# The backward pass of an S4 block: first output finished in the last stage, K's gradient inverted ahead of W2's first parts, and two small preparations moved into the wait for K

## The chip, the cores and the metric

The kernel is one launch on one core of one Trainium2 chip. The metric is device time in microseconds of that launch; the median over the runs shown is compared. TensorE, VectorE, ScalarE, GpSimd and SyncE appear in the profile as PE (PEld for its weight loads), DVE, ACT, POOL and SP.

## The reference

The forward pass is a normalised input, a convolution with a long kernel K made from the parameters of a state space model, and a two-layer feed-forward gate. The kernel returns the forward output and the gradients of eleven inputs for a given `grad_out`.

```python
xn = _layernorm(x)                            # x: 1 x 2048 x 512, bf16
K  = einsum("dn,dnl,dn->dl", C, exp(dt*A*l), dt*B).real        # N = 128 states, l = 0..2047
s  = irfft(rfft(xn, 4096) * rfft(K, 4096))[:2048] + xn * Dskip
g  = silu(silu(xn @ w1) @ w2)                 # w1: 512 x 1792, w2: 1792 x 512
out_0 = x + s * g
out_1 .. out_11 = gradients of x, A_re, A_im, B_re, B_im, C_re, C_im, log_dt, Dskip, w1, w2
```

## The kernel before

Everything works on tiles of 128 partitions. The sequence of 2048 is held as `[128, T=16, 512]` (16 positions to a partition), and the transform of length 4096 is done as matrix products with tables (TF for the forward direction, TI for the inverse, both written to DRAM once and loaded in pieces) and radix-4 additions on VectorE (`rad4`). Spectra have four parts, kt = 0 to 3, each `[128, 2, 4, 512]` (real and imaginary, 1 MB).

The instructions stand in the order in which the Python code issues them; there is no planner. Each engine runs its own list in order, and so does each of the three queues that issue transfers (SyncE, ScalarE, GpSimd); a transfer that waits holds everything behind it on its queue. Pools recycle buffers: a load into a buffer waits for the last reader of what was there. Transfers of SyncE and ScalarE take turns on eight semaphores, so that each also waits for the one eight before it.

- **Stage 1** runs the feed-forward net and makes the tables. It stores the gate's two forms (`gd`, `od`) and fills DS = grad_out * g.
- **Stage 2** makes K through DRAM (`store_K`, `load_K` into `K_b`) and the spectra of xn (`UXd`) and of part 3 of DS. While K's loads are under way it does the last products on VectorE and transposes on TensorE. Its end opens the pools `kq` and `bk3`, starts the generator `gen_kt` and finishes BK3, the part 3 of K's gradient before the inverse.
- **Stage 3** steps `gen_kt`: for each kt, K's spectrum KX (stored to `KXd`), the product with UX, and `rad4` into BY. Beside its first steps it drains `sl`, the transposes of the last slab (`XT`, `YT`). At its end 64 matmuls (L1199) form `ps_dsk`, the sums for Dskip's gradient.
- **Stage 4** inverts BY in eight steps of two (`inv_mm`, L1101). `YOut.load` fetches four operands a step: co, cG, cg, cx. `YOut.pre` makes cG = grad_out times silu' (DSILU on ScalarE, L133, and a product, L1236). `YOut.out` has three VectorE operations: DO_all = S * cG (L1242), S *= cg (L1243), S += cx (L1244), and S_s is stored as out_0 (L1307). Between the steps `gen_d` makes the spectra XD of DS for kt 0 to 2 (stored to `DXd`), the products with UX, and BK0 to BK2. Late in the stage GpSimd loads the first three pieces AW of the hidden layer (`akd`) for W2's gradient, and `Prod` loads KXd and DXd of part 0 (aXl, dXl; L1419, L1421).
- **Stage 5** begins with the selection matrices (`gsum_sel`: iotas on GpSimd, 4 casts and 7 comparisons on VectorE) and three parts of W2's gradient (`Dw2.run`, L1453), which contract over all 16 tiles of DO_all. Then come eight steps of K's inverse (`inv_mm` over BK, `ps_v`), each evicted to dK by ScalarE (L1491) and summed with the selection matrices into `ps_g` (L1485). Beside them VectorE does the products and `rad4` of `Prod` for kt 0 to 3, into BG. The sums go to DRAM (`dKgd`, L1512 and L1513, two buffers `gs_o`) and come back as Gt by GpSimd loads (L1522, L1523). After W2's part 3 and the first three steps of DXC (the inverse of BG), the slabs begin: Gbd (L1606) from Gt and masks, `ps_V` (L1618) with loaded XTl, and so on, between W2's other parts, DXC's other steps and the transposing loads of W2T.
- **Stage 6** goes back through the feed-forward net and ends with W1's gradient: four chunks of `dhd` loaded by GpSimd as dhc (1792 KB each, L1813, two buffers), four sums of 16 matmuls to each (L1840), evicted and stored as o10b.

The step of stage 5 that changes most, as it is written:

```python
    for ft in range(3):
        for _ in w2.run(ft):
            pass
    ...
    for t0 in range(0, T, TS):
        ps = k.pd.tile([P, TS, W], F32, name="ps_v", tag="pd")
        inv_mm(k, ps, k.BK, k.TI.pop(t0), t0, (0, 1, 2, 3))
```

Of the kernel before, what the change touches and what calls it, by code (L numbers as in the profile page):

```python
# [14 lines left out]
P = 128  # L15
# [121 lines left out]
def kernel(ctx, tc, A_u, A_A_re, A_A_im, A_B_re, A_B_im, A_C_re, A_C_im, A_log_dt, A_Dskip, B_x, B_w1, B_w2, grad_out,  # L137
# [16 lines left out]
    LD = lambda nm: dr.tile([L, D], BF16, name=nm)  # L154
    k.gd = LD("gd"); k.od = LD("od")
    k.Kud = dr.tile([NU, D], BF16, name="Kud")
# [775 lines left out]
def stage_2(k):  # L932
# [89 lines left out]
    UX = ld_ux(k, kq, 0)  # L1022
    bk3 = lo.open("bk3")
    gk = gen_kt(k, kq, K_b, UX)
    next(gk)
    k.BK3 = rad_inv(k, bk3, "BK3", PX)
    return gk, sl

# [76 lines left out]
def gsum_sel(k, gp):  # L1105
# [6 lines left out]
    for (v0, st, u0, na, nb, reps, at) in (  # L1112
# [4 lines left out]
        nu = P if nb else 1  # L1117
        ii = gp.tile([P, nu], I32, name=f"gs_i{u0}")
        nc.gpsimd.iota(ii[:], pattern=[[st, nb], [128, na], [8, 16]] if nb else [[0, 1]], base=v0, channel_multiplier=0)
        iv = gp.tile([P, nu], BF16, name=f"gs_v{u0}")  # L1120
        nc.vector.tensor_copy(out=iv[:], in_=ii[:])
# [52 lines left out]
def stage_3(k, gk, sl):  # L1174

    nc = k.nc
    lo, ro = k.left, k.right
    for n, _ in enumerate(gk, 1):
        for g in (next(sl, None) for _ in range(2)):
            if g is not None:  # L1180
                next(g)
        if n == 7:
            ro.close("sb", "xs")
            k.tip = ro.open("tip", 3); k.y2 = ro.open("y2", 2)
            y = k.y = YOut(k)
# [10 lines left out]
    psd = k.psd = k.ps.tile([P, DK, P], F32, name="ps_dsk", tag="pz", bufs=1)  # L1196
    for kt in range(4):
        for t in range(T):
            nc.tensor.matmul(out=psd[:, kt], lhsT=k.DS[:, t, kt * P:(kt + 1) * P], rhs=k.xn[:, t, kt * P:(kt + 1) * P], start=(t == 0), stop=(t == T - 1))  # L1199

# [13 lines left out]
class YOut:  # L1214
# [23 lines left out]
    def out(self, t0, S_s):  # L1238
        k, nc, r = self.k, self.k.nc, self.ins.pop(t0)
        ts_ = slice(t0, t0 + TS)  # L1240
        TT = nc.vector.tensor_tensor
        TT(out=k.DO[:, ts_, :], in0=S_s[:], in1=r["cG"][:], op=ALU.mult)  # L1242
# [9 lines left out]
def gen_d(k, bk, dp):  # L1252
# [4 lines left out]
    for kt in range(3):  # L1257
# [21 lines left out]
def stage_4(k):  # L1279
# [9 lines left out]
    for t0 in range(0, T, TS):  # L1289
# [18 lines left out]
        for _ in range(3 if t0 % 4 else 2):  # L1308
            next(gd, None)
        if t0 == 4:  # L1310
            dskb = dskip_out(k, k.kq)
# [97 lines left out]
class Prod:  # L1409


    def __init__(self, k):
        self.k, self.ld, self.pl = k, {}, [(k.kq, "A", k.kq, "X")]

    def load(self, kt, src):
        k, nc = self.k, self.k.nc
        p0, t0, p1, t1 = self.pl[kt % 2]
        a = p0.tile([P, 2, 4, W], BF16, name="aXl", tag=t0)
        nc.sync.dma_start(a[:], src[kt])  # L1419
        d = p1.tile([P, 2, 4, W], BF16, name="dXl", tag=t1)  # L1420
        nc.sync.dma_start(d[:], k.DXd[kt])  # L1421
        self.ld[kt] = a, d

    def mul(self, kt):
        k = self.k
        a, d = self.ld.pop(kt)
        self.PX = cplx_mul(k.nc, k.mm, a, d, conj_a=True)

    def rad(self, kt, B_):
        k = self.k  # L1430
        t = k.mm.tile([P, 2, 4, W], BF16, name="r4_t", tag="cm_t2")
        E, O = (t[:, i].rearrange("p (c m) w -> p c m w", c=2) for i in range(2))
        rad4(k.nc, B_[:, :, 0:2], B_[:, :, 2:4], self.PX, E, O, True)
# [29 lines left out]
def stage_5(k):  # L1463
# [5 lines left out]
    pr = k.pr  # L1469
    pr.pl.append((k.kq, "UXl", pw, "dXl"))  # L1470
    pr.load(1, k.KXd)
# [16 lines left out]
    for t0 in range(0, T, TS):  # L1488
# [6 lines left out]
        else:  # L1495
            k.TI[t0 + 6 - T] = ld_ti(k, k.tip, t0 + 6 - T)
        kt = (t0 + 2) // 4
        if t0 % 4 == 0:
            pr.rad(kt, BG[:, kt])
        elif kt < 4:  # L1500
            pr.mul(kt)
        if t0 < 4:
            pr.load(t0 // 2 + 2, k.KXd)
        if t0 >= 2:
            gs(t0 - 2)
    gs(T - 2)
    for _ in gen_masks(k, dkp):
        pass
    g0 = k.dKgd[0:256].rearrange("(b p k) d -> k p b d", p=16, k=2)
    for i, (u0, nu, _) in enumerate(sels):  # L1510
        ob = dkp.tile([P, D], BF16, name=f"gs_o{i}", tag=f"gs_o{i % 2}")
        nc.scalar.copy(out=ob[0:nu], in_=(psg + [psz])[i][0:nu])  # L1512
        nc.sync.dma_start(k.dKgd[u0:u0 + nu], ob[0:nu])  # L1513
        if i < 2:
            nc.sync.dma_start(g0[i], dK[0:16, 8 * i:8 * i + 8])
    lo.close("bk", "bk3", "kq")
    S = Slabs(k, lo.open("sw"))
    S.load(0, nc.gpsimd); S.load(1, nc.gpsimd); S.load(2, nc.gpsimd)
    Gt = k.Gt = k.tf2.tile([P, 16, 256], BF16, name="Gt", tag="TFs")
    nc.gpsimd.memset(Gt[64:96], 0.0)  # L1520
    for e in range(2):
        nc.gpsimd.dma_start(Gt[e:79 + e:2], k.dKgd[0:640, 256 * e:256 * e + 256].rearrange("(h l) d -> h l d", l=16))  # L1522
        nc.gpsimd.dma_start(Gt[80 + e:81 + e, 0, :], k.dKgd[640:641, 256 * e:256 * e + 256])  # L1523
    for _ in w2.run(3):
# [269 lines left out]
def stage_6(k):  # L1794
# [5 lines left out]
    k.fx = ro.open("fx", 2)  # L1800
    fb = lo.open("fb", 2)
    B = k.B
    B.fb, B.W1T = fb, W1T
# [31 lines left out]
    for i in range(4):  # L1835
        for dk in range(DK):
# [18 lines left out]
    ro.close("fp4", "ww", "fx", "fw", "wt", "tip", "tf2", "tfp")  # L1855
    lo.close("fb", "do", "mm", "ds")

# [29 lines left out]
```

## Time and profile before

| what | value |
| --- | --- |
| runs | 820.08, 820.78, 816.17 us; median 820.08 |
| profiled execution | 818.51 us, span 816.7 us, mean granted clock 0.925 |
| PE busy | 675.6 us (83%) |
| DVE busy | 623.3 us (76%) |
| ACT busy | 435.4 us (53%) |
| POOL busy | 91.7 us (11%) |
| moved by DMA | 193.09 MB, mean 236 GB/s |
| stage 3 and 4 | about 305 to 460 us |
| K's inverse and sums | 469.4 to 516.1 us |
| first ps_V | 539.8 us |
| W1's sums | 754.8 to 812.8 us |

Busy time is of one execution, and matmuls overlap, so 83% does not mean that TensorE is at its peak. The span runs from the first to the last instruction of the profiled execution; its time is some 2 us longer. In timelines a row gives start, length, engine, line, operation, output<-inputs, count, and in brackets the idle time before it with what ended it. The tile called `ps_w2` or `ps_w1` in the code is `ps_w` in the profile, since numbers are left out.

### The profile page before, as it was taken

To read this page: it belongs to the slowest core of one execution; us is meant where nothing else is said; L and a number is where in the kernel's file an instruction comes from. 1 tells how busy PE (TensorE), PEld (TensorE's weight loads), DVE (VectorE), ACT (ScalarE), POOL (GpSimd) and SP (SyncE) were. 2 spreads that over 40 slices of the span, in tenths; PEclk is the share of its full clock that TensorE was granted. 3 is DMA by queue.
4 is the path that set the end of the run, shared out by engine and by line. 5 is a ranking of instruction groups with operands and counts; after the bars stand their busy time and mean duration, and the time that the engine had idled before them with its cause. 6 is when DMAs were issued, how large, how long until landed. Compare 5 with 4: busy or idle time off the path is not lost.

```text
span 816.7 us, 13686 instructions
## 1 busy us (share of the span) xinstructions
PE 675.6 (83%) x5284; PEld 345.5 (42%) x5284; DVE 623.3 (76%) x1013; ACT 435.4 (53%) x531; POOL 91.7 (11%) x124
## 2 busy tenths in 40 slices
PE   5878969896688557889999579959976899989998
PEld 3434535443456433334444234324433455444454
DVE  6899999639998994999889699745555548988700
ACT  5788888964679464434343112324533675666211
POOL 1251251020000030000000000401022200001010
PEclk9978989998889877989999689979988999999999
DMA  9557767799769499974789788759999597657561
GB/s 280 199 170 260 244 222 264 260 322 290 255 210 279 119 291 278 331 292 174 265 300 350 274 316 282 223 146 271 222 186 265 135 271 217 175 153 233 167 217 50
DMA packets 153806, 193.09 MB, mean 236 GB/s; under 512 B 37179, under 2 KB 114557, under 8 KB 147565
## 3 DMA queue, kind: packets, MB, share of 16 engines
q1 hardware_dynamic: 142780, 156.84, 62.5%
q0 software_dynamic: 6416, 22.30, 8.6%
q10 hardware_dynamic: 4545, 13.08, 5.3%
q8 instruction: 41, 0.67, 0.3%
q14 instruction: 24, 0.20, 0.1%
HBM read 108.01 MB, written 80.50 MB: 231 GB/s over the span
## 4 chain that ended last, share of the span: by engine, by line
PE 25%; DVE 12%; DMA 11%; ACT 4%; SPq 3%; issue 2%; POOL 0%; ACTq 0%; DVEq 0%
PE ps_w L1840 6%; PE ps_v L1101 4%; PE ps_f L1077 4%; DMA XTl<-XTd 3%; PE ps_dx L1763 3%; PE ps_w L1453 2%; PE ps_da L1724 2%; DMA dhd<-dhk 2%; DVE cm_t L106 1%; SPq L1566 1%; DMA dXl<-DXd 1%; PE ps_V L1618 1%; DMA TIs<-TId 1%; DMA TFs<-TFd 1%; ACT sd L133 1%
## 5 line engine op out<-in xcount | busy, mean ns | idle before, releaser
L579 PE MATMUL ps_h<-XNT,W 128*128 128x512 bf16 x224 | 60.3, 418 | 12.2 <-ACT hs L582 12.2
L1453 PE MATMUL ps_w<-DO_all,AW 128*128 128x512 bf16 x224 | 60.4, 421 | 10.2 <-DVE DO_all L1242 10.2
L555 PE MATMUL ps_o<-W,aT 128*128 128x512 bf16 x224 | 56.9, 405 | 2.5 <-DVE ak L76 2.5
L1101 PEld LDWEIGHTS <-TIs 128*128 128x128 bf16 x384 | 37.4, 99 | 49.6 <-issue 6.1
L1077 PEld LDWEIGHTS <-TFs 128*128 128x128 bf16 x304 | 30.4, 102 | 58.6 <-issue 23.6
L1077 PE MATMUL ps_f<-K_b,TFs 128*128 128x512 bf16 x160 | 42.0, 417 | 15.1 <-ACT Ak L1079 7.2
L1724 PE MATMUL ps_da<-DOT,W2T 128*128 128x512 bf16 x224 | 52.9, 379 | 1.5 <-ACT DOT L1704 1.1
L1620 ACT CAST Vb<-ps_V 128x1024 bf16<-128x1024 f32 x32 | 31.8, 1014 | 41.9 <-PE ps_V L1618 24.6
L1763 PE MATMUL ps_dx<-W1T,dhT 128*128 128x512 bf16 x224 | 52.9, 379 | 0.0
L1629 DVE TENSOR_TENSOR T<-Vb,YTl 128x2048 bf16<-128x2048 bf16 x16 | 19.6, 1224 | 42.4 <-ACT Vb L1620 42.4
L1725 DVE TENSOR_TENSOR dhT<-ps_da,sd 128x1024 bf16<-128x1024 f32 x28 | 34.1, 1222 | 23.0 <-ACT sd L133 17.3
L1840 PE MATMUL ps_w<-dhc,xn 128*128 128x448 bf16 x256 | 49.1, 352 | 0.0
L886 ACT COPY XT<-pt_xt 128x1024 bf16<-128x1024 bf16 (+1 forms) x44 | 40.6, 1004 | 5.0 <-issue 3.8
L1453 PEld LDWEIGHTS <-AW 128*128 128x128 bf16 x224 | 21.9, 105 | 44.0 <-issue 25.8
L1618 PE MATMUL ps_V<-XTl,Gbd 82*32 82x256 bf16 x512 | 20.8, 296 | 23.0 <-DMA XTl<-XTd 13.2
L579 PEld LDWEIGHTS <-W 128*128 128x128 bf16 x224 | 22.6, 105 | 37.4 <-issue 20.2
L927 PE MATMUL ps_f<-xn,TFs 128*128 128x512 bf16 x128 | 32.8, 412 | 5.8 <-DMA TFs<-TFd 5.8
L555 PEld LDWEIGHTS <-aT 128*128 128x128 bf16 x224 | 23.3, 104 | 33.6 <-issue 11.1
L1772 ACT ACTIVATE dxn<-dxn,c,rstd 128x512 f32<-128x512 f32 x16 | 13.0, 814 | 43.8 <-DVE c L1771 43.8
L1077 PE MATMUL ps_f<-DS,TFs 128*128 128x512 bf16 x144 | 33.0, 379 | 3.6 <-DMA TFs<-TFd 1.9
L1079 ACT CAST Ak<-ps_f 128x1024 bf16<-128x1024 f32 x16 | 16.0, 1014 | 37.2 <-PE ps_f L1077 21.2
L928 ACT CAST XU<-ps_f 128x1024 bf16<-128x1024 f32 x20 | 20.7, 1040 | 27.5 <-PE ps_f L927 14.5
(299 smaller groups left out, 1545.4 us busy)
## 6 DMA issues: line engine op xcount, KB each, us to landing
TIs<-TId SPq DMA_DIRECT2D x24, 512.0 KB, 7.2
XTd<-XT SPq DMA_DIRECT2D x20, 512.0 KB, 6.1
XTl<-XTd SPq DMA_DIRECT2D x13, 640.0 KB, 6.6
hTd<-hs SPq DMA_DIRECT2D x28, 256.0 KB, 2.4
akd<-ak SPq DMA_DIRECT2D x28, 256.0 KB, 3.7
UXl<-UXd SPq DMA_DIRECT2D x7, 1024.0 KB
hsb<-hTd SPq DMA_DIRECT2D x28, 256.0 KB, 3.2
dhd<-dhk SPq DMA_DIRECT2D x28, 256.0 KB, 5.3
```

Of the source, the lines that this page charges most:

```text
L555: nc.tensor.matmul(out=pso[:], lhsT=aT[:, ft, tt * P:(tt + 1) * P], rhs=W2[:, ft, :], start=(ft == 0), stop=(ft == FT - 1))
L579: nc.tensor.matmul(out=ps[:, j], lhsT=W1[:, dk, ft * P:(ft + 1) * P], rhs=XNT[:, dk], start=(dk == 0), stop=(dk == DK - 1))
L886: nc.scalar.copy(out=XT[:, j0:j0 + len(ks)], in_=pt[:, 0:len(ks)])
L927: nc.tensor.matmul(out=ps[:, c, :], lhsT=TFs[:, t1 + 4 * j, c, :], rhs=src[:, t1 + 4 * j, :], start=(j == 0), stop=(j == 3))
L1077: nc.tensor.matmul(out=ps[:, c, :], lhsT=tab(j), rhs=src[:, t1 + 4 * j, :], start=(n == 0), stop=(n == 4 * len(terms) - 1))
L1101: nc.tensor.matmul(out=ps[:, j, :], lhsT=TIs[:, j, 2 * kt + c, :], rhs=B[kt][:, c, (t0 + j) % 4, :], start=(kt == 0 and c == 0), stop=(kt ...
L1453: nc.tensor.matmul(out=ps[:], lhsT=A[:, t, :], rhs=k.DO[:, t, :], start=(t == 0), stop=(t == T - 1))
L1620: nc.scalar.copy(out=self.V[i][:, g2], in_=ps[:].rearrange("p b c n -> p c b n"))
L1724: nc.tensor.matmul(out=ps[:, j], lhsT=self.W2T[:, dk, ft * P:(ft + 1) * P], rhs=self.DOT[tc_][:, dk], start=(dk == 0), stop=(dk == DK - 1))
L1725: nc.vector.tensor_tensor(out=self.dhT[:, f0:f0 + 2, :], in0=ps[:], in1=sd[:], op=ALU.mult)
L1763: nc.tensor.matmul(out=psx[:], lhsT=dhT[:, ft, t % 4 * P:(t % 4 + 1) * P], rhs=self.W1T[:, ft, :], start=(ft == 0), stop=(ft == FT - 1))
L1840: nc.tensor.matmul(out=ps[:], lhsT=k.xn[:, t, dk * P:(dk + 1) * P], rhs=ch[i][:, t, :], start=(t == 0), stop=(t == T - 1))
```

## The change

1. `YOut` loads co and cG alone, and `out` keeps DO_all; S_s goes to a DRAM tensor `Sd`. A new class `Out0` loads Sd, gd and x again in stage 6 and finishes out_0 there, in eight groups, between the sums of W1's gradient.
2. In stage 5 W2's first three parts are issued after K's inverse, its sums and Gt's loads. The masks follow them. Gt is loaded from SyncE's queue, ahead of the W2 stores, and each `gs_o` has a buffer of its own.
3. `Prod` takes the parts in the order 2, 0, 1, 3. XD of part 2 is still in its buffer and is neither stored nor loaded; its product is issued in stage 4, after BK2.
4. The selection matrices and the whole of Dskip's sums (64 matmuls and the VectorE part) are issued at the end of stage 2, in a new pool `sel`, and the transposes of `sl` begin at the fourth step of `gen_kt` rather than the first.

```diff
@@ stage_2, end
     bk3 = lo.open("bk3")
+    k.sel = lo.open("sel")
+    psd = k.psd = k.ps.tile([P, DK, P], F32, name="ps_dsk", tag="pz", bufs=1)
+    for kt in range(4):
+        for t in range(T):
+            nc.tensor.matmul(out=psd[:, kt], lhsT=k.DS[:, t, kt * P:(kt + 1) * P], rhs=k.xn[:, t, kt * P:(kt + 1) * P], ...)
     gk = gen_kt(k, kq, K_b, UX)
     next(gk)
     k.BK3 = rad_inv(k, bk3, "BK3", PX)
+    k.sels = gsum_sel(k, k.sel)
+    k.dskb = dskip_out(k, k.sel)
@@ stage_3
-        for g in (next(sl, None) for _ in range(2)):
+        for g in (next(sl, None) for _ in range(2 if n >= 4 else 0)):
...
-    psd = ...    (the 64 matmuls)
@@ YOut
-        for nm, src in (("co", k.tl(k.od[:])), ("cG", k.g_v), ("cg", k.tl(k.gd[:])), ("cx", k.x_v)):
+        for nm, src in (("co", k.tl(k.od[:])), ("cG", k.g_v)):
...
         TT(out=k.DO[:, ts_, :], in0=S_s[:], in1=r["cG"][:], op=ALU.mult)
-        TT(out=S_s[:], in0=S_s[:], in1=r["cg"][:], op=ALU.mult)
-        TT(out=S_s[:], in0=S_s[:], in1=r["cx"][:], op=ALU.add)
-        return k.o0_v[:, ts_, :], S_s[:]
+        return k.tl(k.Sd[:])[:, ts_, :], S_s[:]
+class Out0:
+    def load(self, t0):
+        ...
+        for nm, src in (("zS", k.tl(k.Sd[:])), ("zg", k.tl(k.gd[:])), ("zx", k.x_v)):
+            t = self.pool.tile([P, TS, D], BF16, name=nm, tag=nm, bufs=3 if nm == "zS" else 2)
+            k.nc.sync.dma_start(t[:], src[:, t0:t0 + TS, :])
+    def run(self, t0):
+        ...
+        TT(out=S[:], in0=S[:], in1=g[:], op=ALU.mult)
+        TT(out=S[:], in0=S[:], in1=x[:], op=ALU.add)
+        k.nc.sync.dma_start(k.o0_v[:, t0:t0 + TS, :], S[:])
@@ gen_d
+        if kt < 2:
+            nc.sync.dma_start(k.DXd[kt], XD[:])
+        else:
+            k.pr = Prod(k, XD)
         PX = cplx_mul(nc, k.mm, UX, XD, conj_a=True)
-        nc.sync.dma_start(k.DXd[kt], XD[:])
@@ stage_4
         if t0 == 10:
-            store_rows(k, k.kq, k.outs[9], dskb)
+            store_rows(k, k.sel, k.outs[9], k.dskb)
+            k.pr.mul(0)
+            k.pr.load(1)
...
-            k.pr = Prod(k)
-            k.pr.load(0, k.KXd)
-        if t0 + 2 == T:
-            k.pr.mul(0)
@@ Prod
+    order = (2, 0, 1, 3)
+    def load(self, i, pw=None):
+        self.ld[i] = (self.get(k.kq, "A" if i == 2 else "UXl", k.KXd, i), self.get(*((pw, "dXl") if i == 2 else (k.kq, "X")), k.DXd, i))
@@ stage_5
-    sels = gsum_sel(k, dkp)
+    sels = k.sels
...
-    for ft in range(3):
-        for _ in w2.run(ft):
-            pass
...
-        if t0 < 4:
-            pr.load(t0 // 2 + 2, k.KXd)
+        if t0 == 2:
+            pr.load(3)
...
-    for _ in gen_masks(k, dkp):
-        pass
+    Gt = k.Gt = k.tf2.tile([P, 16, 256], BF16, name="Gt", tag="TFs")
+    nc.gpsimd.memset(Gt[64:96], 0.0)
     for i, (u0, nu, _) in enumerate(sels):
-        ob = dkp.tile([P, D], BF16, name=f"gs_o{i}", tag=f"gs_o{i % 2}")
+        ob = dkp.tile([P, D], BF16, name=f"gs_o{i}")
...
+    for e in range(2):
+        nc.sync.dma_start(Gt[e:79 + e:2], k.dKgd[0:640, ...])
+        nc.sync.dma_start(Gt[80 + e:81 + e, 0, :], k.dKgd[640:641, ...])
+    for ft in range(3):
+        for _ in w2.run(ft):
+            pass
+    for _ in gen_masks(k, dkp):
+        pass
     S.load(0, nc.gpsimd); S.load(1, nc.gpsimd); S.load(2, nc.gpsimd)
-    Gt = ...     (memset and four loads on gpsimd)
@@ stage_6, in the loop over W1's sums
+            it = DK * i + dk
+            if it in (2, 3):
+                z.load(2 * it - 4)
+            if 5 <= it < 13:
+                z.run(2 * it - 10)
+            if 5 <= it < 11:
+                z.load(2 * it - 6)
```

More of the change, by code (lines that the diff above doesn't have):

```diff
@@ L1023, in stage_2 @@
     bk3 = lo.open("bk3")
+    k.sel = lo.open("sel")
+    psd = k.psd = k.ps.tile([P, DK, P], F32, name="ps_dsk", tag="pz", bufs=1)
+    for kt in range(4):
+        for t in range(T):
+            nc.tensor.matmul(out=psd[:, kt], lhsT=k.DS[:, t, kt * P:(kt + 1) * P], rhs=k.xn[:, t, kt * P:(kt + 1) * P], start=(t == 0), stop=(t == T - 1))
     gk = gen_kt(k, kq, K_b, UX)
@@ L1195, in stage_3 @@
     k.DO = k.do.tile([P, T, D], BF16, name="DO_all", tag="DO")
[L1196 to L1199, printed above, removed]
 def dskip_out(k, pool):
@@ L1409, with __init__, get, mul @@
 class Prod:
[L1412 to L1424, printed above, removed]
+    order = (2, 0, 1, 3)
+    def __init__(self, k, XD):
+        self.k = k
+        self.ld = {0: (self.get(k.kq, "A", k.KXd, 0), XD)}
+    def get(self, pool, tag, src, i):
+        a = pool.tile([P, 2, 4, W], BF16, name="aXl", tag=tag)
+        self.k.nc.sync.dma_start(a[:], src[self.order[i]])
+        return a
+    def load(self, i, pw=None):
         k = self.k
-        a, d = self.ld.pop(kt)
+        self.ld[i] = (self.get(k.kq, "A" if i == 2 else "UXl", k.KXd, i), self.get(*((pw, "dXl") if i == 2 else (k.kq, "X")), k.DXd, i))
+    def mul(self, i):
+        k = self.k
+        a, d = self.ld.pop(i)
         self.PX = cplx_mul(k.nc, k.mm, a, d, conj_a=True)
-    def rad(self, kt, B_):
+    def rad(self, i, BG):
         k = self.k
+        B_ = BG[:, self.order[i]]
         t = k.mm.tile([P, 2, 4, W], BF16, name="r4_t", tag="cm_t2")
@@ L1469, in stage_5 @@
     pr = k.pr
-    pr.pl.append((k.kq, "UXl", pw, "dXl"))
-    pr.load(1, k.KXd)
-    sels = gsum_sel(k, dkp)
+    pr.load(2, pw)
+    sels = k.sels
     w2 = k.w2
@@ L1496, in stage_5 @@
             k.TI[t0 + 6 - T] = ld_ti(k, k.tip, t0 + 6 - T)
[L1497 removed]
+        i = (t0 + 2) // 4
         if t0 % 4 == 0:
[L1499 to L1503 removed]
+            pr.rad(i, BG)
+        elif i < 4:
+            pr.mul(i)
+        if t0 == 2:
+            pr.load(3)
         if t0 >= 2:
@@ L1515, in stage_5 @@
             nc.sync.dma_start(g0[i], dK[0:16, 8 * i:8 * i + 8])
-    lo.close("bk", "bk3", "kq")
+    for e in range(2):
+        nc.sync.dma_start(Gt[e:79 + e:2], k.dKgd[0:640, 256 * e:256 * e + 256].rearrange("(h l) d -> h l d", l=16))
+        nc.sync.dma_start(Gt[80 + e:81 + e, 0, :], k.dKgd[640:641, 256 * e:256 * e + 256])
+    for ft in range(3):
[3 more added lines that the diff above has]
+        pass
+    lo.close("bk", "sel", "bk3", "kq")
     S = Slabs(k, lo.open("sw"))
     S.load(0, nc.gpsimd); S.load(1, nc.gpsimd); S.load(2, nc.gpsimd)
[L1519 to L1523, printed above, removed]
     for _ in w2.run(3):
@@ L1801, in stage_6 @@
     fb = lo.open("fb", 2)
+    z = Out0(k, lo.open("oz", 2))
     B = k.B
```

22 lines of the change are left out of this document (14 added, 8 removed).

## The prediction

> **What bounds the kernel now.** I read the page first, then the chain of waits, the windows by stretch, TensorE's timeline around the moved lines, and the list of DMA issues.
>
> ```profile
> span 816.7 us, 13686 instructions
> ...
> PE 25%; DVE 12%; DMA 11%; ACT 4%; SPq 3%; issue 2%; POOL 0%; ACTq 0%; DVEq 0%
> ```
>
> No engine holds the whole chain; it must be read by stretch (us, busy us of PE, PEld, DVE, ACT, POOL, granted clock, DMA share, GB/s):
>
> ```profile
> 418.00:446.00 28.00, 28.00 (x131) 12.59 (x130) 25.82 (x36) 10.52 (x12) 1.57 (x3) 1.00 0.87 322
> 446.00:460.00 14.00, 3.79 (x14) 1.32 (x13) 13.48 (x21) 3.10 (x3) 1.10 (x7) 0.69 0.66 210
> 460.00:470.00 10.00, 10.00 (x37) 4.02 (x35) 2.36 (x3) 1.17 (x2) 0.07 (x1) 0.76 0.96 360
> 530.00:540.00 10.00, 0.24 (x7) 0.14 (x10) 0.93 (x2) 1.02 (x1) 1.89 (x3) 0.66 0.69 176
> 585.00:646.00 61.00, 47.26 (x469) 20.73 (x470) 30.94 (x42) 26.54 (x31) 10.83 (x20) 0.89 0.90 193
> 782.00:786.00 4.00, 4.00 (x23) 2.06 (x21) 0.00 (x0) 0.99 (x2) 0.00 (x0) 1.00 1.01 390
> 786.00:790.00 4.00, 4.00 (x23) 2.06 (x21) 0.00 (x0) 0.61 (x2) 1.15 (x1) 1.00 0.13 39
> ```
>
> TensorE is full in stage 4 up to 446, then stands still twice: 446 to 460, while VectorE is full, and 530 to 540, while nothing computes. After each the granted clock is low. TensorE's timeline and the chain give the reasons:
>
> ```profile
> 456.57 1.01 PE L1453 MATMUL ps_w<-DO_all,AW 128*128 128x512 bf16 x2 [7.32 <-DVE DO_all L1242]
> 459.42 10.17 PE L1453 MATMUL ps_w<-DO_all,AW 128*128 128x512 bf16 x34 [1.84 <-DVE DO_all L1242]
> 469.42 7.07 PE L1101 MATMUL ps_v<-BK,TIs 128*128 128x512 bf16 x32
> ```
> ```profile
> 458.89 9.44 DMA dXl<-DXd
> ...
> 516.03 7.55 DMA dKgd<-gs_o
> 525.64 3.44 DMA ldt<-in_A_log_dt_dram
> ...
> 531.38 7.46 DMA Gt<-dKgd
> 539.07 0.70 DVE Gbd L1606
> ```
>
> W2's first parts wait for the last DO_all; K's inversion stands behind them; the Gt round trip (store, load) then has too little TensorE work beside it. The rows that price transfers:
>
> ```profile
> TIs<-TId SPq DMA_DIRECT2D x24, 512.0 KB, 7.2
> ...
> dhc<-dhd POOLq DMA_DIRECT2D x4, 1792.0 KB, 9.8
> ...
> AW<-akd POOLq DMA_DIRECT2D x3, 512.0 KB, 8.6
> ```
>
> **The change part by part**, against the profiled execution: span 816.7, 818.51 with what lies around it, 1.57 under the median 820.08. Times are the trace's; minus is a gain.
>
> *Before stage 4: -1.6.* VectorE idles 10.6 us up to 325.4, for K_b. Selection matrices (475.2 to 479.7, 4.5) and Dskip's sums (424.4 to 425.8, 1.5) fit there: 314.8 + 6.0 = 320.8. Dskip's 64 matmuls (3.77) go into TensorE's idle before 311.4. The transposes between K's last two sums move behind them: two sums of 8 matmuls (1.73 each) and two evictions end at 323.8 rather than 325.4. Bounds 0 and -2.5.
>
> *Dskip's matmuls leave 366.8 to 370.6: +0.4.* VectorE holds the chain there, so nothing is gained; TensorE's idle before 379.4 grows from 1.75 to about 5. After 3.24 idle (at 346.2) matmuls start 0.43 apart instead of 0.22, so some 8 run late, 1.7 us, mostly inside the wait for BY at 389.0. Bounds 0 and +1.7.
>
> *Stage 4's loads: -1.4.* The loads of cg and cx go (4 MB; stores to Sd replace those to out_0). The table load at 408.7 took 8.6 against a shortest of 6.0 and cost TensorE 1.9 at 417.4. Bounds 0 and -1.9. So TensorE's last Y inversion ends at 445.4 - 2.6 = 442.8.
>
> *K's inversion ahead of W2: -10.0.* With the 2.6 taken off: S_s of step 8 is evicted at 433.3, then VectorE does DO_all (0.7, to 434.0), XD (2.4), product (6.8), cG and DO_all (1.4), rad (4.9, BK2 at 449.5), row (0.2). The 16 operations of the output (0.7 each, 11.2 in all) are gone, but only the four before BK2's rad that lie behind TensorE's eviction help, 2.8. K's first inversion step thus ends near 453, not 472.9. The second does not follow at once. SyncE's queue is in order: the load of dXl (step 1) overwrites XD and waits until the moved product has read it (449.7 + 2.3 + 1.1 + 1.1 = 454.3), and TIs of step 2 stands behind it: issued 454.8, landed 7.2 later, 462.0. TensorE has nothing else and cools: 3.6 + 1.7 + 1.3 (sums) gives step 4 at 468.6, against 483.15. From there to the sums' end took 32.9 (to 516.06) with 1.1 lost to a slow clock: now 500.4. Product and rad chains (6.85 and 4.9) end at about 500 too. Then three W2 parts start after an eviction (0.7) and take 3 x 3.46, to 511.5; the fourth's AW is loaded only after the first part (505.1 + 8.1 = 513.2); W2 and three DXC steps, 4 x 3.5, end at 527.2. Gt: four evictions of 0.57 with a buffer each (the third waited 7.2 for a store before), to 503; stores 4 to 7.5; four issues (1.6), now on SyncE; landing 7.5: by 520, hidden; past 527.2 every us counts. Behind the waiting Gt on SyncE stand only W2's stores and TIs that are read after 530. Moved on POOL: the masks' three iotas (0.13 to 0.16) behind Gt's memset (3.5), and with them XTl, near 500; VectorE's masks (7.8) end at 508. Keeping XD saves a store and a load of 1 MB. The first ps_V starts at 527.2 against 539.81: -12.6, of which -2.6 is booked. Bounds -5 (TIs and AW at 12 us) and -14 (at 4.0, the shortest TIs).
>
> *From there to 640: 0.* Same work, same order, shifted. The waits there are for XTl and W2's transposes behind SyncE; nothing new is queued. But the DMA share is 0.90, so up to +4.
>
> *Stage 6: +3.0.* 24 loads and 8 stores of 256 KB come in; 16 VectorE operations (0.69) cost nothing, VectorE being idle from 778. The danger is dhc, whose third load is issued on POOL at 778.24 and is needed at 773.19 + 5 x 3.03 = 788.35; DMA is quiet again from 786 on, so it landed with some 1.7 to spare. It needs about 3.7 plus 1.835 MB at the 390 GB/s of the row above, 4.7. Six new groups of loads are issued from the sixth of W1's sixteen sums (L1840) on (779.3), one each 3.03 (two more before). Beside a full SyncE queue, the three AW loads of POOL (1.5 MB in about 9 to 10) got half of the 322 GB/s of their stretch. At half, dhc takes 3.7 + 9.4 = 13.1, lands 791.3 and holds TensorE 3.0. The fourth is then needed at 803.5 and, issued at 788.8, lands at 801.9. The SyncE queue's backlog (about 6.8 MB after 779) clears near the end; o10b has three buffers. Bounds 0 and +8. The Trainium skill (DMA: Bandwidth & Descriptors, Specifications) gives about 358 GB/s as a core's HBM limit; the trace shows 390, so the row is used. By the page dhc would take 13.9 and the stall would be 3.8.
>
> Sum: -1.6 + 0.4 - 1.4 - 10.0 + 3.0 = -9.6: 808.9 for the profiled execution, 820.08 - 9.6 = 810.5 on the median.
>
> **The rivals.**
> *No stall in stage 6, 807.8.* For: POOL's queue moves 22.30 MB in 6416 packets (3.5 KB), SyncE's 156.84 MB in 142780 (1.1 KB). If turns go by packets, dhc gets 70% or more: 3.7 + 6.7 = 10.4, a stall of 0.3, -12.3 in all; quick TIs and AW take it towards 803. Against: AW's half. The Trainium skill (same page, Queues, rings and completion order) says that each engine takes turns between queues packet by packet; no run here isolates it.
> *Given back, 817.* The DMAs are the bound from 500 to 640: the same bytes in 12 us less. Two thirds lost there leaves -3.
> *The queue holds K's inversion, 819.* If SyncE stands at dXl until about 468 (product late, or its own load late), step 2 starts near 473 as before and only the filled Gt wait stays, which stage 6 takes back. Against: aXl of the product is issued at about 436, 13 us ahead.
> *Slower: dhc starves, 829.* The program lets a SyncE transfer start once the eighth before it has landed, so up to 2 MB are in flight; if they go first, dhc moves only what is left. TensorE has no other work, so each us past 788.35 counts. At 1.835 MB in 32 us (57 GB/s) it lands at 810: +21.7 - 12.6 = +9. The sum turns positive once dhc needs more than 10.1 + 12.6 = 22.7 us. For: a load of 512 KB on POOL took 11.2 earlier, 47 GB/s. Against: dhc and AW ran at 160 or more.
>
> **How the numbers follow.** Forecast 0.55 (own range 806 to 815); no stall 0.17; given back 0.12 (of it 0.02 below 816); queue holds 0.05; slower 0.11. A measurement of this kernel tells about 0.5% (4.1 us) from no change: faster 0.55 + 0.17 + 0.02 = 0.74, same 0.10 + 0.05 = 0.15, slower 0.11. The range 803 to 821 leaves out the slower case and a little below.
>
> **What would show it.** Right: VectorE busy from 315 to 321; ps_v<-BK starting before 455 with a gap of 6 to 10 us between its first and second step, ended by TIs, and SyncE's dXl waiting for VectorE's L108; ps_V starting near 527 with no wait for Gbd; a wait of TensorE at the ninth of W1's sixteen sums, ended by dhc. Wrong: ps_V later than 535, XTl waits grown by over 5 us, or dhc landing over 18 us after its issue.

## The result and the profile after

The changed kernel has a median of 811.24 us over 20 runs (807.43 to 820.43), the kernel before, run beside it, 818.55 us over 20 (813.14 to 824.30). The ratio is 0.9921, with a 95% interval of 0.9901 to 0.9941: faster by 0.8%, some 6.5 us, where the prediction summed to 9.6. The first profiled execution of the change was a slow one (820.43 us, at a lower clock), so the lines below are of a second one, 814.37 us with a span of 812.3 (the run `again` further down), and in the table the slow one's values stand in brackets and count in no mean. The bounds, as the page has them:

```profile
span 812.3 us, 13705 instructions
...
PE 33%; DMA 19%; DVE 18%; ACT 10%; issue 4%; SPq 1%; ACTq 0%; DVEq 0%; POOLq 0%
```

The windows of the stretches that the change touches (same columns as before: us, busy us of PE, PEld, DVE, ACT, POOL, granted clock, DMA share, GB/s):

```profile
446.00:460.00 14.00, 5.29 (x16) 1.83 (x16) 13.86 (x17) 3.10 (x3) 0.00 (x0) 0.77 0.58 193
460.00:470.00 10.00, 7.21 (x24) 2.90 (x25) 9.79 (x12) 1.02 (x1) 0.00 (x0) 0.65 0.99 385
505.00:520.00 15.00, 10.63 (x41) 4.28 (x40) 3.59 (x26) 0.92 (x2) 0.58 (x1) 0.83 0.84 250
530.00:540.00 10.00, 9.32 (x97) 4.40 (x96) 3.19 (x5) 5.70 (x7) 0.00 (x0) 1.00 0.95 308
790.00:796.00 6.00, 2.88 (x14) 1.23 (x12) 1.39 (x2) 0.53 (x1) 0.00 (x0) 0.90 1.00 364
```

The hole of 530 to 540 is gone (TensorE 9.32 of 10 us, 0.24 before). In its place there are two smaller ones, around 455 to 463 and 512 to 516, with granted clocks of 0.65 (460 to 470) and 0.83 (505 to 520), and a new one around 792; in these three windows the DMA's share is 0.84 to 1.00. TensorE's timeline shows what ended each:

```profile
446.47 1.04 PE L1108 MATMUL ps_v<-BK,TIs 128*128 128x512 bf16 x4 [1.65 <-DMA TIs<-TId]
450.36 4.26 PE L1108 MATMUL ps_v<-BK,TIs 128*128 128x512 bf16 x12 [2.85 <-DVE BK L97]
462.79 5.73 PE L1108 MATMUL ps_v<-BK,TIs 128*128 128x512 bf16 x16 [8.18 <-DMA TIs<-TId]
...
501.09 10.53 PE L1480 MATMUL ps_w<-DO_all,AW 128*128 128x512 bf16 x48
515.98 6.43 PE L1480 MATMUL ps_w<-DO_all,AW 128*128 128x512 bf16 x16 [4.37 <-DMA AW<-akd]
522.25 10.52 PE L1108 MATMUL ps_v<-BG,TIs 128*128 128x512 bf16 x48
532.71 0.62 PE L1644 MATMUL ps_V<-XTl,Gbd 82*32 82x256 bf16 x16
```

K's inverse starts at 446.5, not 469.4, and its sums end at 501.2, not 516.1. Of these 15 us, 7.1 are left at the first ps_V (532.7 against 539.8). Behind the sums stand now W2's first three parts (10.53), a wait of 4.37 for AW and the fourth part, whose 16 matmuls take 6.43 rather than some 3.5. Gone is the wait that the kernel before had there for Gbd, 9.76 us:

```profile
519.74 10.31 PE L1101 MATMUL ps_v<-BG,TIs 128*128 128x512 bf16 x47
539.81 1.04 PE L1618 MATMUL ps_V<-XTl,Gbd 82*32 82x256 bf16 x16 [9.76 <-DVE Gbd L1606]
```

The last stage has a wait that was not there. The last 13 of W1's sums before, and then in the change:

```profile
773.19 39.51 PE L1840 MATMUL ps_w<-dhc,xn 128*128 128x448 bf16 x208
```

```profile
764.35 27.40 PE L1867 MATMUL ps_w<-dhc,xn 128*128 128x448 bf16 x144
794.88 13.88 PE L1867 MATMUL ps_w<-dhc,xn 128*128 128x448 bf16 x64 [3.12 <-ACT o10b L1869]
```

It is easier to compare stretches than whole runs. Each row is a difference of two times in one profile; W1's sums are taken from the end of the matmuls before them.

| stretch | before (2 profiles) | change | variants that keep the edit |
| --- | --- | --- | --- |
| last wait for K's load, to the eviction of Y's second half step | 83.5, 83.9 | (83.9) 84.7 | 83.3 to 84.8, mean with the change 83.9 |
| from there to the end of Y's inverse | 50.6, 50.0 | (48.6) 48.6 | 48.6 to 49.8 |
| end of Y's inverse to the first ps_V | 94.4, 96.5 | (87.8) 87.9 | 86.6 to 87.8 |
| first to last ps_V | 99.5, 93.1 | (98.5) 97.7 | 90.5 to 94.4; 97.3 and 97.7 with other loads of the slabs |
| hidden layer's gradient up to W1's first sum | 111.6, 111.6 | (111.6) 111.6 | 111.6, once 112.2 |
| W1's last 13 sums | 39.4, 39.3 | (46.2) 44.2 | 45.0 to 46.2 |

So the change wins some 7.5 us between Y's inverse and the slabs and 1.8 in stage 4, and loses some 6 in the last stage (4.9 in the profile shown, more in the variants) and 0.5 in stage 3.

### The profile page after: what moved, and what is told of

The parts are those of the page before. It is cut to its first block, busy times and chain, and to the rows that moved or that the text cites. A ratio compares the mean times of both kernels' runs of the same rounds, so it can differ in the third digit from the quotient of the medians.

```text
span 818.4 us, 13636 instructions
## 1 busy us (share of the span) xinstructions
PE 674.7 (82%) x5215; PEld 347.7 (42%) x5284; DVE 623.5 (76%) x1013; ACT 434.9 (53%) x531; POOL 89.6 (11%) x120
## 4 chain that ended last, share of the span: by engine, by line
PE 41%; DMA 16%; DVE 15%; ACT 8%; issue 4%; SPq 1%; ACTq 0%; another core or an unknown queue 0%; DVEq 0%
PE ps_v L1108 8%; PE ps_f L1084 6%; PE ps_w L1480 4%; DMA XTl<-XTd 3%; PE ps_w L1867 3%; PE ps_da L1750 3%; DMA K_b<-Kud 3%; PE ps_f L927 3%; PE ps_dx L1789 3%; PE ps_o L555 2%; PE ps_V L1644 2%; DMA dhd<-dhk 2%; PE ps_k L814 1%; DMA AW<-akd 1%; DMA out_dram<-o10b 1%
## 5 line engine op out<-in xcount | busy, mean ns | idle before, releaser
L579 PE MATMUL ps_h<-XNT,W 128*128 128x512 bf16 x212 | 60.1, 428 | 14.5 <-ACT hs L582 13.9
L1480 PE MATMUL ps_w<-DO_all,AW 128*128 128x512 bf16 x213 | 55.2, 409 | 6.0 <-DMA AW<-akd 4.3
L1867 PE MATMUL ps_w<-dhc,xn 128*128 128x448 bf16 x256 | 51.5, 363 | 4.5 <-ACT o10b L1869 4.5
L555 PE MATMUL ps_o<-W,aT 128*128 128x512 bf16 x221 | 53.0, 385 | 1.9 <-DVE ak L76 1.7
L1084 PE MATMUL ps_f<-K_b,TFs 128*128 128x512 bf16 x155 | 39.7, 404 | 15.2 <-DMA K_b<-Kud 7.9
L1108 PE MATMUL ps_v<-BK,TIs 128*128 128x512 bf16 x126 | 32.4, 411 | 13.0 <-DMA TIs<-TId 11.0
L1084 PE MATMUL ps_f<-DS,TFs 128*128 128x512 bf16 x142 | 35.5, 402 | 5.5 <-ACT dEO L1086 5.4
L1867 PEld LDWEIGHTS <-xn 128*128 128x128 bf16 x256 | 25.7, 100 | 29.8 <-issue 4.6
```

The lines of the kernel that those rows point to most:

```text
L555: nc.tensor.matmul(out=pso[:], lhsT=aT[:, ft, tt * P:(tt + 1) * P], rhs=W2[:, ft, :], start=(ft == 0), stop=(ft == FT - 1))
L579: nc.tensor.matmul(out=ps[:, j], lhsT=W1[:, dk, ft * P:(ft + 1) * P], rhs=XNT[:, dk], start=(dk == 0), stop=(dk == DK - 1))
L1084: nc.tensor.matmul(out=ps[:, c, :], lhsT=tab(j), rhs=src[:, t1 + 4 * j, :], start=(n == 0), stop=(n == 4 * len(terms) - 1))
L1108: nc.tensor.matmul(out=ps[:, j, :], lhsT=TIs[:, j, 2 * kt + c, :], rhs=B[kt][:, c, (t0 + j) % 4, :], start=(kt == 0 and c == 0), stop=(kt ...
L1480: nc.tensor.matmul(out=ps[:], lhsT=A[:, t, :], rhs=k.DO[:, t, :], start=(t == 0), stop=(t == T - 1))
L1867: nc.tensor.matmul(out=ps[:], lhsT=k.xn[:, t, dk * P:(dk + 1) * P], rhs=ch[i][:, t, :], start=(t == 0), stop=(t == T - 1))
```

## The experiments

Ratios are to the kernel before, with 95% intervals. For effects under 1% these intervals overlap, so the stretches of the profiles carry most verdicts.

**again** is the changed kernel once more, with no edit.

> The changed kernel as it is, for a second profile and as a base on the same chip. Expected 0.990 to 0.994 of the kernel before (some 810 to 813 us). In the profile of the change TensorE stood 4.5 us before the last four of W1's sums, released by an eviction o10b that had waited for its store; its eighth of K's inverse had a gap of 8.4 us in front of the second step. Theory A: both belong to the program and return here within 1 us. Rival: they belong to that one execution and shrink below 2 us.

0.9935 (0.9898 to 0.9971). The gap behind K's first step came back (8.18 us): theory A. The one in W1's sums came back smaller (3.12 us, and 1.6 more for a slow clock behind it), which is neither within 1 us nor below 2: its size differs from one execution to the next.

**no_z** stores the unfinished S_s to out_0:

```diff
-        return k.tl(k.Sd[:])[:, ts_, :], S_s[:]
+        return k.o0_v[:, ts_, :], S_s[:]
...   (and no z.load, z.run in stage 6)
```

> Leaves out the finishing of out_0: S_s is stored to out_0 as it is, and the 24 loads, 8 stores and 16 VectorE operations of the last stage are gone. Theory A (the last stage pays for them: W1's sums took 64.9 us from first to last against 58.0 before): faster than the change by 5 to 7 us, 804 to 807, W1's sums without a gap in about 58 us. The prediction's own term would make it 3.0. Rival (what the last stage waits for is there anyway, as in the kernel before with its quiet DMA): faster by under 2 us.

0.9814 (0.9759 to 0.9868), median 805.04. W1's last 13 sums took 39.3 without a gap, as before the change: theory A. So the last stage pays 4.9 for finishing out_0 in the change's profile (44.2), and up to 6.8 in the variants that keep it (46.2 in ti_first). The rest of this run's gain lies between the first and last ps_V (92.6 us against 97.7), which no_z does not touch.

**st_pool** takes the stores of o10b off SyncE's queue:

```diff
             if pend:
-                nc.sync.dma_start(*pend.pop())
+                nc.gpsimd.dma_start(*pend.pop())
```

> The stores of o10b go to GpSimd's queue, so that they no longer stand behind the loads and stores of out_0 on SyncE's. Theory A (the gap in W1's sums comes from o10b's three buffers, which wait for stores in SyncE's queue): faster than the change by 4 to 7 us, the gap before the last four sums gone. Theory B (the prediction's: the transfers share the bandwidth, whatever the queue): within 2 us of the change, and the wait returns as one for dhc or for o10b.

0.9904 (0.9868 to 0.9939). That is some 2.5 us less than `again`, between the two theories, and the intervals do not tell the two runs apart. The stretch fell to 41.2, so 3.1 of the 4.9 went with the stores of o10b off that queue. ScalarE's timeline of the change shows how they cost: with three buffers, an eviction waits until an earlier store on SyncE, issued among the transfers of out_0, has landed.

```profile
785.55 0.53 ACT L1869 CAST o10b<-ps_w 128x448 bf16<-128x448 f32 x1 [3.39 <-DMA out_dram<-o10b]
794.29 0.53 ACT L1869 CAST o10b<-ps_w 128x448 bf16<-128x448 f32 x1 [8.21 <-DMA out_dram<-o10b]
```

With that wait gone, TensorE of st_pool meets the one that the prediction had named, at the thirteenth sum:

```profile
788.05 12.28 PE L1867 MATMUL ps_w<-dhc,xn 128*128 128x448 bf16 x64 [1.65 <-DMA dhc<-dhd]
```

In the change itself dhc stands right behind the stores. This is its fourth load on GpSimd's queue, which the thirteenth sum needs:

```profile
781.43 1.16 POOL L1840 DMA_DIRECT2D dhc<-dhd  x1 [12.44 <-DMA out_dram<-o10b]
```

It landed 12.37 us later, at 793.80; the twelfth sum had ended at 791.75, and the eviction of 794.29 at 794.83. So of the 3.12 us some 2.0 would have been there without the stores of o10b. In four variants with the same wait (3.8 to 4.4 us) dhc was 2.3 to 3.1 late.

**ti_first** loads the tables ahead of the second product's operands:

```diff
             k.pr.mul(0)
-            k.pr.load(1)
+        if t0 + 2 == T:
+            k.pr.load(1)
```

> The load of aXl and dXl for the second product is issued after the tables TIs of K's second and third inversion step, not ahead of them. Theory A (dXl waits for the first product and holds TIs): the gap of 8.4 us before the second step falls below 3, and the first ps_V comes 5 to 8 us earlier; 803 to 807 if nothing behind it takes it back. Rival 1 (the loads of W2's fourth part, XTl or Gt take it back): gap gone, first ps_V or the stretch up to 640 gives back more than half, 808 to 811. Rival 2 (the product, whose load now comes later, becomes what the sums and the first DXC steps wait for): within 1 us or slower.

0.9929 (0.9893 to 0.9964). The gap before the second step shrank to 1.83, and one before the fourth opened; from the start of K's inverse to the end of its sums 54.5 us, 54.7 in the change. No theory had placed it: what was won was lost two steps later.

```profile
457.61 3.63 PE L1108 MATMUL ps_v<-BK,TIs 128*128 128x512 bf16 x16 [1.83 <-DMA TIs<-TId]
462.37 3.62 PE L1108 MATMUL ps_v<-BK,TIs 128*128 128x512 bf16 x16
472.78 6.34 PE L1108 MATMUL ps_v<-BK,TIs 128*128 128x512 bf16 x16 [5.50 <-DMA TIs<-TId]
```

The DMA moves 374 GB/s from 455 to 480 in this run, at a share of 0.94, and 361 in the change, at 0.93. The order on SyncE decides which step waits. That the bytes themselves set the sum of the waits fits both rows; no run here took bytes away.

**w2_first** undoes only the reordering of W2:

```diff
+    for ft in range(3):
+        for _ in w2.run(ft):
+            pass
     psg = [k.ps.tile([P, D], F32, name=f"ps_g{i}", tag="ps") for i in range(3)]
...   (and not behind Gt's loads)
```

> Puts W2's first three parts back ahead of K's inverse; all else as changed. The time from the end of Y's last inversion to the first ps_V was 94.4 us before and 87.9 in the second profile of the change. Theory A (the reordering of W2 and K's inverse is what brings this): the stretch goes back to 92 to 96 and the kernel is 5 to 8 us slower than the change. Rival (the kept XD, the missing S_s work and Gt on SyncE bring it, and the order is worth little): the stretch stays below 90, the time within 2 us of the change.

0.9959 (0.9923 to 0.9994). The stretch from Y's inverse to ps_V became 90.2: between the two expectations. By this one profile the reordering alone is worth 2.3 us on top of the rest (the profiles that leave this stretch alone lie within 1.3 of each other, the two of before 2.1 apart); the other 4 to 6 of that stretch come with the other edits.

**prep_old** puts the transposes, Dskip's matmuls and its VectorE part back:

```diff
-        for g in (next(sl, None) for _ in range(2 if n >= 4 else 0)):
+        for g in (next(sl, None) for _ in range(2)):
...   (psd's 64 matmuls at the end of stage_3, dskip_out at t0 == 4)
```

> Undoes two pieces of the fourth edit: the transposes of the last slab begin at the first step of gen_kt again, and Dskip's 64 matmuls and its VectorE part return to the end of stage 3 and to stage 4. The selection matrices stay where the change put them. The first Y inversion step ended at 394.8 us before, at 396.2 in the change, where the prediction had 393.6. Theory A (both edits cost more by TensorE's clock than they bring: K's first 17 matmuls took 6.48 us instead of 5.45, and DS's sums 7.31 instead of 4.48 behind 5.4 us of idle): that step ends at 394 to 395, 1 to 2 us earlier than with the change. Rival (the shift is the load of K and differs from run to run): counted from the first sum behind the load of K, nothing changes by more than 0.5 us.

0.9935 (0.9903 to 0.9967). The absolute time moved with the load of K (the last wait for it ended anywhere from 310 to 315 in these profiles), so the first expectation's 394 to 395 was of no use: 396.7. The total is that of `again`. Counted from K's load, the step took 83.3, against a mean of 83.9 with the edits and of 83.5 in the six profiles without. TensorE's rows of the change and of prep_old show one part of it:

```profile
379.41 7.31 PE L1084 MATMUL ps_f<-DS,TFs 128*128 128x512 bf16 x20 [5.42 <-ACT dEO L1086]
```
```profile
381.30 4.26 PE L1079 MATMUL ps_f<-DS,TFs 128*128 128x512 bf16 x19 [1.53 <-ACT dEO L1081]
```

Without Dskip's 64 matmuls TensorE is idle 5.4 us, and the 20 matmuls behind run at a lower clock. From the end of BY on VectorE to the eviction of Y's second half step takes 5.6 to 6.2 in the profiles with the edits and 4.7 in the six without. From the start of K's last sums to VectorE's first r_t the change is 1.4 faster (means 13.0 and 14.5), but VectorE's chain from there to BY is 0.8 longer (65.0 and 64.3). So the net is 0.5 to 0.6, half of what theory A had and at the rival's bound; the two parts of opposite sign, 1.1 lost here and 0.6 won ahead of it, are clearer than their sum.

**w2_gap** fills the gap with W2's first two parts:

```diff
+        if t0 == 0:
+            for ft in range(2):
+                for _ in w2.run(ft):
+                    pass
+            psg += ...; psz = ...
...
-    for ft in range(3):
-        for _ in w2.run(ft):
-            pass
+    for _ in w2.run(2):
+        pass
```

> Issues W2's first two parts between K's first and second inversion step, where TensorE waits 8 us for TIs; the third stays behind K's sums. Theory A (the wait there is one for data that TensorE can fill, and the fourth part's AW then comes early): the two parts take 6.9 us of the gap, K's sums end at about 501 as now or 1 us earlier for a warm clock, the wait of 4.4 us for AW and the slow clock behind it (2.8) go, and the first ps_V comes 5 us earlier, no more since Gt lands about 6 us before it is needed now: 805 to 809. Rival 1 (the DMA is full from 460 to 480, at 380 GB/s: two more AW loads push TIs out): K's sums end 3 us or more later and nothing is won. Rival 2 (Gt, whose stores take 15 us, becomes the wait, as in the kernel before): first ps_V at 528 to 531, with a wait for Gbd.

0.9912 (0.9881 to 0.9943), median 809.70. The gap is used, and the wait for AW is gone. Two waits ended the gain: 4.00 for an eviction on ScalarE, which stood at a load of AW, and, as rival 2 had it, 4.07 for Gbd. First ps_V at 529.9, 86.5 behind Y's inverse. Gt was late since its stores took long: from the issue of the first store to that of Gt's first load 17.7 us, and 18.0 in the change, whose SyncE timeline shows both:

```profile
501.06 0.32 SPq L1536 DMA_DIRECT2D dKgd<-gs_o  x1
...
519.03 0.85 SPq L1540 DMA_DIRECT2D Gt<-dKgd  x1
```

**z_early** finishes out_0 beside the hidden layer's gradient:

```diff
+        if n in (6, 8):
+            z.load(n - 6)
+        if 10 <= n < 26 and n % 2 == 0:
+            z.run(n - 10)
+            z.load(n - 6)
...   (and no z.load, z.run between W1's sums)
```

> Out_0 is finished in the same stage but earlier, one group with every second step of the hidden layer's gradient (n = 10 to 24), not between W1's sums. Theory A (the price of the last stage is the SyncE queue and the DMA full of z in its last 40 us, 4.9 us; the 112 us ahead of it are bound by TensorE and have room): the last 13 sums take 39.4 us again, the stretch ahead grows by less than 2, and the kernel is 3 to 5 us faster than the change. Rival (VectorE's 11 us and the loads delay dhT and hsb, on which TensorE waits): the stretch ahead, 111.6 us, grows by 5 us or more.

0.9948 (0.9913 to 0.9982). W1's last sums took 39.5, but the stretch ahead 119.7: the rival. The longest of TensorE's waits there (us in all, times, longest), in the change and in z_early:

```profile
PE pt_dh L1772 <- DVE dhT L1751: 3.6, 5, 1.0
```
```profile
PE pt_dh L1772 <- DVE dhT L1751: 7.6, 5, 2.2
```

These are 4.0 of the 8.1 us; waits for dhk and DOT hold 2.1 more, and the rest is not placed.

**before_again** is the kernel before, unedited.

> The kernel before, for a second profile of it. In its first one the stretch from the first to the last ps_V took 99.5 us; nine profiles of the changed kernel and its variants had 91.6 to 98.5, mean 94.1. Theory A (the order ahead of the stretch changes it, some 5 us): 98 or more again. Rival (the XTl loads there differ from execution to execution, the mean is the same): 91 to 96.

One run, 814.68 us. The first to the last ps_V took 93.1, the rival's value; the longest waits there are for XTl in all kernels.

**parts23** keeps the second and third edit only:

```diff
...   (out_0 finished in YOut.out; transposes, Dskip and gsum_sel where they were before; no pool sel)
```

> Only the second and third edit on the kernel before: K's inverse ahead of W2, Gt on SyncE, the parts in the order 2, 0, 1, 3. Out_0 is finished in stage 4 as before, and the selection matrices, Dskip's sums and the transposes are where they were. Theory A (part by part: out_0's move wins 2.0 us in stage 4 and loses 4.9 to 6.8 in the last stage, the small preparations lose 0.5): 3 to 5 us faster than the change, near 0.987 of the kernel before, the last 13 sums in 39.4 us, stage 4's last seven inversion steps in 50.6. Rival (the prediction: out_0's VectorE work, back in stage 4, delays BK2 by 2.8 us and the first ps_V with it, the sum of the moves near zero): within 2 us of the change, and the time from the end of Y's last inversion to the first ps_V 2 us or more longer than the change's 87.9.

0.9947 (0.9915 to 0.9979): the rival. Out_0's move and the small preparations are together worth no more than the measurement can tell, though the last sums took 39.3 and stage 4 50.4, as theory A had it. From Y's inverse to ps_V it took 93.8: K's first step waited 4.0 for TIs, its second began 20.3 behind Y's inverse (18.0 in the change), and there are three more waits of 0.6 to 1.9, two for TIs and one for the selection matrices. What the last stage pays, this stretch had won.

**combo** is w2_gap, st_pool and prep_old with one more edit:

```diff
-    S.load(0, nc.gpsimd); S.load(1, nc.gpsimd); S.load(2, nc.gpsimd)
+    S.load(0, nc.gpsimd); S.load(1); S.load(2)
```

> What the runs so far point to, put together on the changed kernel: W2's first two parts in the gap behind K's first inversion step, the o10b stores on GpSimd's queue, transposes and Dskip's sums where they were before, and of the first three slabs' loads only the first ahead of Gt on GpSimd's queue, the other two behind Gt on SyncE's. Theory A (each cause is its own): the stores of dKgd take 8 us instead of 15, no wait for Gbd, first ps_V some 82 us behind the end of Y's last inversion (change: 87.9), last 13 sums in 41 us; 8 to 10 us faster than the change, 0.980 to 0.984 of the kernel before. Rival 1 (the slabs' loads, later now, are waited for instead): the stretch of ps_V grows by 3 us or more. Rival 2 (Gt's stores are slow for their small pieces, not for what runs beside them): a wait of 3 to 5 us for Gbd stays, 0.985 to 0.989.

0.9844 (0.9806 to 0.9883), median 804.53: faster than both kernels, just above theory A's range. In the middle it won more than theory A had: first ps_V 77.1 us behind Y's inverse. Gt's stores and loads in its SyncE timeline, 7.0 apart and not 18.0:

```profile
503.91 0.32 SPq L1542 DMA_DIRECT2D dKgd<-gs_o  x1
...
510.91 0.85 SPq L1546 DMA_DIRECT2D Gt<-dKgd  x1
```

The 2.7 MB of the three slabs, issued at about the same time, had delayed the stores: w2_gap, with the same order of W2 and all three slabs ahead, has 17.7. Rival 1 shows as well: from first to last ps_V it took 97.7 against 94.4 in w2_gap, with a wait of 3.4 for TIs that no other run has there. And the last stage took 47.1 where theory A had 41; the wait there is now the one for dhc, with a slow clock behind it:

```profile
769.22 12.28 PE L1872 MATMUL ps_w<-dhc,xn 128*128 128x448 bf16 x64 [0.56 <-DMA dhc<-dhd]
785.65 14.96 PE L1872 MATMUL ps_w<-dhc,xn 128*128 128x448 bf16 x64 [4.15 <-DMA dhc<-dhd]
```

On GpSimd's queue dhc has the stores of o10b ahead of it. Its fourth load was issued 4.0 us after the eighth sum had ended (at 768.66), 1.8 in the change; a store that waited for its eviction stood in front until 771.15:

```profile
770.61 0.54 POOL L1888 DMA_DIRECT2D out_dram<-o10b  x1 [6.55 <-ACT o10b L1874]
772.66 1.18 POOL L1845 DMA_DIRECT2D dhc<-dhd  x1 [1.52 <-PE ps_w L1872]
```

**combo2** gives out_0 to GpSimd at z_early's places, and the two slabs' loads go behind conv(2):

```diff
-            k.nc.sync.dma_start(t[:], src[:, t0:t0 + TS, :])
+            k.nc.gpsimd.dma_start(t[:], src[:, t0:t0 + TS, :])
-        TT = k.nc.vector.tensor_tensor
+        TT = k.nc.gpsimd.tensor_tensor
```

> The combination again, with two differences. Out_0 is finished at the places of z_early (n = 10 to 24), but by GpSimd, loads, products, sums and stores, where VectorE's 11 us held dhT and cost TensorE 8.1 us; the o10b stores are on SyncE's queue as in the change. And the loads of the second and third slab stand behind the first two DXC steps, whose TIs they delayed (a wait of 3.4 us). Theory A (z_early's price was VectorE's time, the last stage's price the transfers beside W1's sums): the stretch of the hidden layer's gradient stays at 111.6 to 113, the last 13 sums take 39.4, 7 us less than in the combination, and the kernel is some 797 us, 0.973 to 0.978 of the kernel before. Rival 1 (the loads, or GpSimd's work beside VectorE's, slow the stretch all the same): it grows by 5 us or more, and nothing is won over the combination's 804.5. Rival 2 (GpSimd is so slow that dhc behind it on its queue comes late): a wait of TensorE for dhc at the first of W1's sums.

1.0140 (1.0091 to 1.0189), median 829.91: slower, rival 1. W1's last sums took 39.3, but the stretch of the hidden layer's gradient 141.9, 30 more. GpSimd had no step to wait for: it worked from 635.7 to 692.6, in part beside the transposing loads of W1T (issue of one 2.6 us in the median, 1.4 in the change), on which TensorE then waited 11.2. TensorE's waits for dhT grew by 6.6 as well, those for dhk by 4.1. With the slabs' loads behind conv(2) the wait for TIs is gone, but those for XTl grew from 7.8 to 11.9, and from first to last ps_V it took 97.3. And VectorE's small operations grew. The groups by form (count, busy us, mean ns) of combo2, and then of the change:

```profile
L1803 DVE TENSOR_SCALAR c<-m,rstd 128x2 f32<-128x2 f32 x3 | 6.8, 2277 | 0.1
L1802 DVE SCALAR_TENSOR_TENSOR ln_t<-dxn,xn 128x512 f32<-128x512 f32 x3 | 3.8, 1254 | 0.1
```
```profile
L1796 DVE SCALAR_TENSOR_TENSOR ln_t<-dxn,xn 128x512 f32<-128x512 f32 x6 | 4.2, 692 | 0.2
L1797 DVE TENSOR_SCALAR c<-m,rstd 128x2 f32<-128x2 f32 x6 | 1.4, 228 | 0.2
```

## Why the prediction was right in its sign, and where its terms were off

- *Before stage 4, -1.6: measured -0.6.* The work fitted into VectorE's idle time as said (314.1 to 320.5, forecast 314.8 to 320.8), and r_t comes 1.4 earlier after K's load. What the term left out is VectorE's chain behind it, which grew by 0.8 (means 65.0 and 64.3). That the moved transposes lengthen it was not tried by itself; prep_old, which puts them and Dskip's part back, has 64.4.
- *Dskip's matmuls, +0.4: measured +1.1.* Mechanism right to the number (idle 5.42, forecast about 5). The wait for BY hid less of the slow clock than was assumed; the upper bound of 1.7 was the nearer end.
- *Stage 4's loads, -1.4: measured -1.8, and -1.5 as a mean over the ten profiles with this edit.* Right; the wait for TFs (1.9 and 1.3 before) is gone in the change, and three variants keep 0.6 to 1.0 of it.
- *K's inversion, -10.0: measured -6.5 to -8.6, depending on the profile of before.* Up to the end of K's sums the working held: from the end of Y's inverse 56.3 us, forecast 57.6, with the gap of 8.2 us ended by TIs and dXl held 3.8 us for VectorE's L108, as said. (ti_first shows that this order tells where the gap falls, not what it costs: with TIs ahead of dXl the waits were 1.83 and 5.50, and the sums ended no earlier.) The step that failed comes after: "the fourth's AW is loaded only after the first part (505.1 + 8.1 = 513.2)", a wait of 1.7. AW landed at 516.0 (wait 4.37), and TensorE ran its 16 matmuls in 6.43, not 3.46; together 5.6, about what the first ps_V is late (532.7, forecast 527.2). The prediction said that XTl's loads move to "near 500" but gave them no price. combo, which moves two of the three slabs, brings Gt's loads from 17.7 (w2_gap) to 7.0 us behind the first store. That these loads also delayed AW was not tried by itself. Of Gt's cover, "stores 4 to 7.5" and "by 520, hidden" were wrong as well: Gt's loads were issued 18.0 us after the first store, and Gt was in at 526.5, still hidden, by some 4 us.
- *And what the gain of that stretch is due to* was told wrongly. The prediction gave 2.8 of it to the work that leaves VectorE and most to the order. w2_first puts 2.3 on the order, and parts23 shows that the second and third edit without the rest bring 0.6 to 2.7. The other 5.9 (93.8 to 87.9) came with the first and fourth. That it is the work off VectorE and the loads out of stage 4 fits the waits of parts23; which of these does more was not tried.
- *From there to 640, 0.* Open. Two profiles of before gave 99.5 and 93.1, nine of the change and its variants with their loads of the slabs unaltered 90.5 to 97.7, mean 93.2. A gain of some 3 us is possible, a loss is not seen.
- *Stage 6, +3.0: measured +4.9 in the change, mean of five profiles +6.0.* The sign and the cause (out_0 finished there) are shown by no_z, but the wait was another. TensorE did not wait for dhc at the ninth sum: that load took 10.6 us, where the sum had 13.1 and the rival without a stall 10.4. The sum had read its half of the DMA from AW's whole time, issue to landing, and then added 3.7 of fixed time once more. The line "o10b has three buffers" priced the stores at nothing; at the thirteenth sum their wait ended last. dhc came second, but close: by its landing alone TensorE would have stood 2.0 of the 3.12 us, at the load of which the prediction said that it would be in time ("lands at 801.9", needed at 803.5). It was the wait once the stores were moved away (st_pool 1.65, combo 4.71).

Put together, -0.6 + 1.1 - 1.8 - 7.5 + 6.0 is -2.8, and with some -3.0 (93.2 against the mean of 99.5 and 93.1) between the first and last ps_V -5.8; the ratio of the first 20 runs says -6.5, that of `again` -5.3. So about two thirds of the sum's 9.6 came. That the median came out at 811.24, close to the forecast's 810.5, is in part luck: the kernel before, with more runs, has 818.55 and not 820.08, and the gain that was not forecast, between the first and last ps_V, made up for a part of what the two wrong steps lost.

## What to carry to other kernels

When work is moved out of a full stretch into one that looks empty, price every buffer whose store or load goes through the same queue there, not only the transfer that is nearest to its due time: the chain of three small output buffers, which had no price, ended last, and the one that had a price stood right behind it. When a stall is filled, list the loads that now start earlier as well; here they hit the next stage's inputs. And before an order of steps is credited with a gain, undo the order alone: by the one profile here it brought a third of what the stretch gained.

## What the runs showed of the hardware that was not expected

- A GpSimd operation beside VectorE makes some VectorE operations wait out most of it: a 128x2 tensor_scalar took 2.28 us and not 0.23 while GpSimd's 128x1024 tensor_tensor took 2.1, and a 128x512 scalar_tensor_tensor with two operands in SBUF 1.25 and not 0.69. dhT's product, with one operand in PSUM, stayed at 1.22. The Trainium skill (SBUF — State Buffer, SBUF: two separate sides) describes a port pair that VectorE and GpSimd share, locked for a whole instruction, which a VectorE operation needs in a two-port mode, or with two SBUF inputs while the GpSimd operation reads SBUF. The last two rows agree with it; that the tensor_scalar, with one tensor input, was in a two-port mode no run here shows.
- Stretches with the same code differ by 5 to 6 us from one execution to the next: the first to the last ps_V of the kernel before 99.5 and 93.1, the end of the last wait for K's load 310.1 to 314.9 in seven profiles whose code is the same up to there. A single pair of profiles, read without that, puts such a difference down to the change.
- dhc held its own beside SyncE's full queue. Between the first and last packet of the ninth sum's load the DMA moved 387 GB/s, 270 of them dhc's (70%); for the thirteenth's it was 217 of 351 (62%). This is near the 70% that the prediction worked out for turns by packets and above its half. By the Trainium skill (DMA: Bandwidth & Descriptors, Queues, rings and completion order) an engine takes turns between queues packet by packet. The shares agree with that, but no run here varies the packets. The 358 GB/s of the Specifications there in the Trainium skill is no bound in this kernel: 460 to 470 has 385.
